# Attention, low-rank mixer and feed-forward on one core: the first batch's mixer moved a stage later, loads and DMA transposes moved earlier, and some transposes moved to TensorE

## The chip, the cores and the metric

The kernel runs on one core of a Trainium2 chip. The metric is device time in microseconds (us). Each timed comparison runs the kernel before and the variant on the same chip, in rounds. Here "slow" means more than 1.5% above the fastest run of the same kernel. The experiments ran on four chips (e1 to e4 on one, e5 to e8, e9 to e11 and e12 on others); the kernel before, timed again on each, had medians between 281.69 and 282.17 us, so a difference between runs of two chips carries about 0.5 us of doubt besides the spread. The engines are called PE (TensorE matmul), PEld (TensorE weight load), DVE (VectorE), ACT (ScalarE), POOL (GpSimd) and SP (SyncE, which here only issues DMAs).

## The reference

Four batches of eight-head attention over 768 positions, head size 64. Each query keeps 96 local positions and 8 global ones. The output, 768 x 512 per batch, goes through a rank-32 mixer along the sequence and a feed-forward block of width 2048.

```python
scores = scale * q @ k.T + bias;  scores = where(keep, scores, -1e9)
x = softmax(scores) @ v                      # (B, S, 512), heads side by side
h = x.transpose(0, 2, 1) @ U @ V             # U: 768x32, V: 32x768
u = x + h.transpose(0, 2, 1)
out = u + maximum(u @ w_ch1, 0) @ w_ch2      # w_ch1: 512x2048, w_ch2: 2048x512
```

## The kernel before

It works on 16 *pairs* of heads, four per batch. For pair i it needs: q and k transposed; `kP`, a copy of k in which 32 of each block's 128 positions are the global ones; `vp`, the same for v; scores, exp and mask; the products with v (`ob`); the mixer (`tmp_ps`, then `h_ps`, then `uu`, which is u in fp16); and `uT`, u transposed, for the feed-forward (`hps` then `cps`). Feed-forward work is cut into chunks of 512 tokens and queued. In the main loop (pairs 4 to 15) `fill(f)` takes f items of four products from the queue and puts them between the attention steps. In the traces here each engine takes its instructions in the order of the program (in the kernel before, GpSimd's `kP` copy of pair 5 starts only at 53.9 us, after the two loads listed ahead of it, at 51.66 and 52.47). So the place of a line decides what stands behind what.

Pairs 0 to 5 have q and k transposed by TensorE. Pairs 6 to 15 have it done by DMA transposes, issued on SP, from natural-layout staging tiles `qkn`. GpSimd issues all loads from DRAM; they convert fp32 to fp16.

```python
stg = stp.tile([P, NSB, 2, D], FP16, name="qkn", tag="qkn", bufs=4)
# v_prev: blocks of v with the global rows in front
if i < 2:  nc.vector.tensor_copy(vp, vh[:, :, 0:NPB]); ...   # VectorE
else:      nc.sync.dma_start(vp[G:P], vh[G:P, :, 0:NPB]); ...  # DMA, SBUF to SBUF
# ... cut ...
for i in range(NPAIR, NP):             # main loop, pairs 4..15
    v_prev(i + 2)
    scores(i + 1, 0);  fill(f)
    av(i);  norm(i)
    transposes(i + 2, 0);  fill(f)     # DMA transpose of q
    scores(i + 1, 1);  cast_x(i);  fill(f)
    mask(i + 1, 0);  mix_tmp(i);  fill(f)
    scores(i + 1, 2);  fill(f)
    mix_h(i, nc.vector);  mask(i + 1, 1)
    transposes(i + 2, 1);  k_prev(i + 2, nc.gpsimd);  fill(f)
    if i % 2 == 0 and i + 4 < NP:  load(i + 4, 2)
    fill(f)
    mix_t(i)                           # DMA transpose of u
    if i % NPAIR == NPAIR - 1:  queue_batch(i // NPAIR)
    fill(f)
while mlp_q:  fill(1)
```

The softmax here doesn't subtract the row's maximum and nothing guards it: scores larger than these inputs give would overflow.

Of the kernel before, what the change touches and what calls it, by code (L numbers as in the profile page):

```python
# [9 lines left out]
FP32 = mybir.dt.float32  # L10
# [7 lines left out]
def kernel(  # L18
# [27 lines left out]
    NPAIR = H // 2  # L46
    TT = 512
    D1 = D + 1
    KEEP = False
    DT = True  # L50
    assert NG <= G and NL <= P - G + 1 and NPAIR == NDC
    qk_scale = 1.0 / math.sqrt(D)
# [28 lines left out]

    w1_16 = big.tile([P, NDC, DFF], FP16, name="w1_16")
    w2_16 = big.tile([P, NJC, DM], FP16, name="w2_16")
    uT = big.tile([P, NDC, B * S], FP16, name="uT")
    VR = 8
    VPR = 3
    v16 = big.tile([P, VR, 2, NSB, D1], FP16, name="v16")
# [28 lines left out]
    def load_qk_natural(i):  # L116
        b, hp = divmod(i, NPAIR)
        for which, src in enumerate((q, k)):
            stg = stp.tile([P, NSB, 2, D], FP16, name="qkn", tag="qkn", bufs=4)
            for hi in range(2):  # L120
                nc.gpsimd.dma_start(  # L121
                    stg[:, :, hi],
                    src[b, 2 * hp + hi].rearrange("(n p) d -> p n d", p=P),
                )
            stage[i, which] = stg

    def load(i0, n):
        if DT and i0 >= NSTART:
            for j in range(n):
                load_qk_natural(i0 + j)  # L130
        else:
            load_qk(i0, n)
        load_v(i0, n)

    w1v = moe_w_ch1.rearrange("(c p) n -> p c n", p=P)
    w2v = moe_w_ch2.rearrange("(c p) n -> p c n", p=P)
# [48 lines left out]
        relf, relf, 0.5 - NL, BIG, op0=ALU.is_lt, op1=ALU.mult,  # L185
    )
    nc.vector.tensor_tensor(r12, r12, relf, ALU.add)
    nc.vector.tensor_copy(rel3[:, 0], rel3[:, 1])
    nc.vector.tensor_scalar_max(rel3[0:NG, 0], rel3[0:NG, 1], float(-NL))
    nc.vector.memset(rel3[0:G, 2], BIG)  # L190
    nc.vector.memset(rel3[0:NG, 2], float(-NL))
    expb = cst.tile([P, H, 3, P], FP16, name="expb")

    def masks_of(hp):
# [2 lines left out]



    def keep_busy(bank, n):  # L200
        for _ in range(n if KEEP else 0):
            nc.tensor.matmul(bank, zz[:, 0:P], zz, start=True, stop=True)

    qTs, kTs, kPs = {}, {}, {}
    probs = {}
# [5 lines left out]
    def transposes(i, which):  # L211
        if i >= NP:
            return
        stg = stage.pop((i, which))
        if DT and i >= NSTART:
            dst = qkp.tile([P, NSB, P], FP16, name="qkT", tag="qT" if which == 0 else "kT")
            nc.sync.dma_start_transpose(dst, stg.rearrange("p n h d -> p (n h d)"))
            if which == 0:
                qTs[i] = dst.rearrange("p n c -> p (n c)")
            else:  # L220
                kTs[i] = dst
            return
        if i < NSTART:
            bank = ps_mm("tpb")
            keep_busy(bank, 8 if i == 0 and which == 0 else 1)
            tp = bank.bitcast(FP16)[:, 0:NSB * P]
        else:
            tp = ps_tp("tp", FP16, NSB * P)
        for sb in range(NSB):
            for hi in range(2):  # L230
                nc.tensor.matmul(  # L231
                    tp[64 * hi:64 * hi + 64, sb * P:(sb + 1) * P], stg[:, hi, sb],
                    ident16, is_transpose=True,
                    start=(sb == 0), stop=(sb == NSB - 1),
                )
        tv = tp.rearrange("p (n c) -> p c n", n=NSB)
        if which == 0:
            qT = qkp.tile([P, S], FP16, name="qT", tag="qT")
            nc.scalar.activation(qT.rearrange("p (c n) -> p c n", n=NSB), tv, AF.Copy)
            qTs[i] = qT  # L240
        else:
            kT = qkp.tile([P, NSB, P], FP16, name="kT", tag="kT")
            ko = kT.rearrange("p n c -> p (n c)").rearrange("p (c n) -> p c n", n=NSB)
            if i == 0:
                nc.vector.tensor_copy(ko, tv)
            else:
                nc.scalar.activation(ko, tv, AF.Copy)
            kTs[i] = kT
# [10 lines left out]
    def v_prev(i):  # L259
        if i >= NP:  # L260
            return
        vh = v16[:, i % VR]
        vp = vp16[:, i % VPR]
        if i < 2:
            nc.vector.tensor_copy(vp, vh[:, :, 0:NPB])
            nc.vector.tensor_copy(vp[0:G], vh[0:G, :, 0:1].broadcast_to((G, 2, NPB, D1)))
        else:
            nc.sync.dma_start(vp[G:P], vh[G:P, :, 0:NPB])
            for hi in range(2):
                nc.sync.dma_start(  # L270
                    vp[0:G, hi], vh[0:G, hi, 0:1].broadcast_to((G, NPB, D1))
                )
# [5 lines left out]
    def scores(i, ci):  # L278
        if i >= NP:
            return  # L280
        qT, kT, kP = qTs[i], kTs[i], kPs.get(i)
        if ci == 0:
            probs[i] = epp.tile([P, 2, NBK, P], FP16, name="ep", tag="ep")
        ep = probs[i]
        idx = CH[ci]
        n = len(idx)
        scs = [ps_sc("sc") for _ in range(2)]
        if i < NPAIR:
            keep_busy(scs[0], 1)
        for j, bi in enumerate(idx):  # L290
            prev, t = ORDER[bi]
            for hi in range(2):
                r = slice(64 * hi, 64 * hi + 64)
                lhsT = kP[r, t - 1] if prev else kT[r, t]
                nc.tensor.matmul(  # L295
                    scs[hi][:, j * P:(j + 1) * P], lhsT, qT[r, t * P:(t + 1) * P],
                    start=(j == 0), stop=(j == n - 1),
                )
        for hi in range(2):
            nc.scalar.activation(  # L300
                ep[:, hi, idx[0]:idx[0] + n].rearrange("p n c -> p (n c)"),
                scs[hi][:, 0:n * P], AF.Exp, scale=qk_scale,
            )
# [89 lines left out]
    def mix_t(i):  # L393
        b, hp = divmod(i, NPAIR)
        uu = u16s.pop(i)
        if DT and i >= NPAIR:
            nc.sync.dma_start_transpose(
                uT[:, hp, b * S:(b + 1) * S].rearrange("p (n c) -> p n c", n=NSB),
                uu.rearrange("p n c -> p (n c)"),
            )  # L400
            return
        tpu = ps_tp("tpu", FP16, S)
        for st in range(NSB):
            nc.tensor.matmul(
                tpu[:, st * P:(st + 1) * P], uu[:, st], ident16, is_transpose=True,
                start=(st == 0), stop=(st == NSB - 1),
            )
        nc.vector.tensor_copy(uT[:, hp, b * S:(b + 1) * S], tpu)

    mlp_q = deque()  # L410

    def queue_chunk(ci):
        htr = ffp.tile([P, NJC, TT], FP16, name="htr", tag="htr")
        t0 = ci * TT

        def mk_jt(jt):
            def go():
                hh = ps_mm("hps")
                for dc in range(NDC):
                    nc.tensor.matmul(  # L420
                        hh, w1_16[:, dc, jt * P:(jt + 1) * P], uT[:, dc, t0:t0 + TT],
                        start=(dc == 0), stop=(dc == NDC - 1),
                    )
                if jt % 2 == 0:
# [7 lines left out]
        def mk_tt(tt, part):  # L432
# [13 lines left out]
                    nc.sync.dma_start(out[b, n * P:(n + 1) * P, :], osb)  # L446
            return go

        for jt in range(NJC):
            mlp_q.append(mk_jt(jt))  # L450
        for tt in range(TT // P):
# [6 lines left out]
                mlp_q.popleft()()  # L458


    transposes(0, 0)
    transposes(0, 1)
    masks_of(0)
    k_prev(0, nc.vector)
    scores(0, 0)
    transposes(1, 0)
    scores(0, 1)
    transposes(1, 1)
    mask(0, 0)
    scores(0, 2)  # L470
    masks_of(1)
    k_prev(1, nc.vector)
    v_prev(0)
    mask(0, 1)
    for i in range(NPAIR):
        last = i == NPAIR - 1
        v_prev(i + 2)
        scores(i + 1, 0)
        av(i)
        norm(i)  # L480
        scores(i + 1, 1)
        cast_x(i)
        mask(i + 1, 0)
        if i == 0:
            v_prev(1)
        transposes(i + 2, 0)
        if i > 0:
            mix_t(i - 1)
        mix_tmp(i)
        scores(i + 1, 2)  # L490
        if last:
            mix_h(i, nc.vector)
            mask(i + 1, 1)
            transposes(i + 2, 1)
            k_prev(i + 2, nc.gpsimd)
            mix_t(i)
        else:
            transposes(i + 2, 1)
            k_prev(i + 2, nc.vector if i == 0 else nc.gpsimd)
            mask(i + 1, 1)  # L500
            mix_h(i, nc.vector)
            if i + 2 < NPAIR:
                masks_of(i + 2)
        if i == 0:
            load(4, 2)
        if i == 1:
            load_w2()
        if i == 2:
            load(6, 2)

    def queue_batch(b):
        for ci in range(B * S // TT):
# [5 lines left out]
    for i in range(NPAIR, NP):  # L518
        if i % NPAIR == 0:
            f = max(1, len(mlp_q) // (8 * NPAIR))  # L520
        v_prev(i + 2)
        scores(i + 1, 0)
        fill(f)
        av(i)
        norm(i)
        transposes(i + 2, 0)
        fill(f)
        scores(i + 1, 1)
        cast_x(i)
        fill(f)  # L530
        mask(i + 1, 0)
        mix_tmp(i)
        fill(f)
        scores(i + 1, 2)
        fill(f)
        mix_h(i, nc.vector if DT else nc.gpsimd)
        mask(i + 1, 1)
        transposes(i + 2, 1)
        k_prev(i + 2, nc.gpsimd)
        fill(f)  # L540
        if i % 2 == 0 and i + 4 < NP:
            load(i + 4, 2)
        fill(f)
        mix_t(i)
        if i % NPAIR == NPAIR - 1:
            queue_batch(i // NPAIR)
        fill(f)
# [37 lines left out]
```

## Time and profile before

| quantity (kernel before) | value |
|---|---|
| time | 280.97 us median of the first three runs |
| stage 1, to the second scores of pair 5 | 54.8 us |
| stage 2, attention mixed with feed-forward | 55 to 220 us |
| stage 3, the last 256 feed-forward products | 220 to 276 us, 216 ns each |
| TensorE waits in stage 2, summed | about 23 us |

The first view is the table of busy time in chosen stretches, kernel before. The columns are the stretch, its length, then for PE, PEld, DVE, ACT and POOL the busy us and the number of instructions, then the granted clock, DMA share and GB/s.

```profile
core 0: us, PE busy (x) PEld busy (x) DVE busy (x) ACT busy (x) POOL busy (x), PEclk, DMA share, GB/s
13.00:55.00 42.00, 31.01 (x390) 21.28 (x390) 26.54 (x50) 26.20 (x48) 15.87 (x20) 0.92 1.47 190
55.00:220.00 165.00, 142.06 (x1123) 67.18 (x1120) 85.75 (x138) 58.81 (x107) 41.41 (x56) 0.99 0.87 104
220.00:280.00 60.00, 55.94 (x253) 24.52 (x252) 16.60 (x24) 9.55 (x16) 0.00 (x0) 0.99 0.11 40
```

In stage 1 no compute engine is full, and the DMA share is above 1 (transfers overlap). In stage 2 TensorE is busy for 142 of 165 us, and no other engine comes close, so the 23 us it lacks are what a change can win. Stage 3 is full.

The next view is the chain of waits, kernel before, at the end of stage 1: start, length, what.

```profile
33.37 18.01 DMA w_16_82<-in_moe_w_ch_dram
51.38 0.28 issue
51.66 0.70 POOL qkn L121
52.36 0.11 issue
52.47 1.43 POOL v_84 L110
53.91 0.59 POOL kP L255
54.50 0.26 POOL kP L256
...
54.80 0.33 PE sc L295 x4
```

The scores wait for `kP`. `kP` stands on GpSimd behind a load, and the issue of that load waits until the second half of w2 has landed. The load does not use w2; w2 is only the load that was issued eight places earlier.

The third view is the TensorE timeline, kernel before, cut to some waits of stage 2: start, length, engine, line, operation, output and inputs, shapes, count, and in brackets the idle time before it and what ended it.

```profile
66.06 0.40 PE L295 MATMUL sc<-qkT 64*128 64x128 f16 x8 [2.79 <-DMA qkT<-qkn]
...
91.50 0.52 PE L295 MATMUL sc<-qkT 64*128 64x128 f16 x8 [3.55 <-DMA qkT<-qkn]
91.95 1.89 PE L438 MATMUL cps<-w_16_82,htr 128*128 128x512 f16 x4
...
98.20 0.29 PE L367 MATMUL tmp_ps<-x_1302,u_106 128*32 128x128 f16 x6 [0.93 <-ACT x_1302 L359]
...
106.19 1.24 PE L420 MATMUL hps<-uT,w_16_81 128*128 128x512 f16 x5 [0.99 <-DMA uT<-uu]
...
220.24 1.02 PE L420 MATMUL hps<-uT,w_16_81 128*128 128x512 f16 x4 [1.24 <-DMA uT<-uu]
```

The change aims at three families of waits: for transposed q/k, for the cast of x on ScalarE, and for transposed u. (A fourth, for results that ScalarE and VectorE must first take away, `htr`, is about 5 us and stays.) After the 3.55 us wait four products took 1.89 us, at a granted clock of 0.50 between 92 and 94 us; undisturbed groups of four took 1.04. Below, "cold" means such products at the half clock.

### The profile page before, as it was taken

To read this page: it belongs to the slowest core of one execution; us is meant where nothing else is said; L and a number is where in the kernel's file an instruction comes from. 1 tells how busy PE (TensorE), PEld (TensorE's weight loads), DVE (VectorE), ACT (ScalarE), POOL (GpSimd) and SP (SyncE) were. 2 spreads that over 40 slices of the span, in tenths; PEclk is the share of its full clock that TensorE was granted. 3 is DMA by queue.
4 is the path that set the end of the run, shared out by engine and by line. 5 is a ranking of instruction groups with operands and counts; after the bars stand their busy time and mean duration, and the time that the engine had idled before them with its cause. 6 is when DMAs were issued, how large, how long until landed. Compare 5 with 4: busy or idle time off the path is not lost.

```text
span 280.0 us, 4506 instructions
## 1 busy us (share of the span) xinstructions
PE 234.0 (84%) x1832; PEld 116.4 (42%) x1832; DVE 134.0 (48%) x226; ACT 100.6 (36%) x180; POOL 68.9 (25%) x96
## 2 busy tenths in 40 slices
PE   2567786976785898999999999678989899999994
PEld 1355564433342444444444444334444344444441
DVE  4366657363644263735457345455665332223221
ACT  2776665343541325433064230446321131013100
POOL 8930436405440534052402423111000000000000
PEclk9999998699999799999999999999999999999999
DMA  8999999977994999597593985954113200120011
GB/s 85 160 196 215 188 194 199 135 66 124 112 129 117 147 136 136 51 156 80 117 135 82 127 74 137 119 109 81 28 46 97 66 2 0 75 76 2 0 75 75
DMA packets 99796, 29.08 MB, mean 104 GB/s; under 512 B 88256, under 2 KB 96192, under 8 KB 99776
## 3 DMA queue, kind: packets, MB, share of 16 engines
q0 software_dynamic: 62736, 13.73, 55.9%
q1 hardware_dynamic: 37040, 15.07, 24.8%
q8 instruction: 14, 0.23, 0.3%
q14 instruction: 6, 0.05, 0.1%
HBM read 27.46 MB, written 6.29 MB: 121 GB/s over the span
## 4 chain that ended last, share of the span: by engine, by line
PE 59%; DMA 15%; ACT 11%; DVE 7%; POOL 3%; issue 2%; SPq 2%; DVEq 0%; ACTq 0%; POOLq 0%
PE cps L438 24%; PE hps L420 24%; DMA w_16_82<-in_moe_w_ch_dram 6%; ACT ep L300 6%; PE sc L295 4%; DMA uT<-uu 3%; DMA qkT<-qkn 3%; DVE x_sb L386 2%; DMA qkst<-in_q_dram 2%; DVE ep L313 2%; PE ob L333 2%; PE ob L337 2%; PE tmp_ps L367 1%; PE h_ps L381 1%; ACT htr L425 1%
## 5 line engine op out<-in xcount | busy, mean ns | idle before, releaser
L420 PE MATMUL hps<-uT,w_16_81 128*128 128x512 f16 x384 | 93.8, 384 | 8.2 <-DMA uT<-uu 3.4
L438 PE MATMUL cps<-w_16_82,htr 128*128 128x512 f16 x384 | 89.7, 382 | 0.0
L300 ACT ACTIVATE ep<-sc 128x512 f16<-128x512 f32 (+1 forms) x96 | 48.8, 561 | 85.2 <-PE sc L295 85.2
L420 PEld LDWEIGHTS <-w_16_81 128*128 128x128 f16 x384 | 35.2, 98 | 49.8 <-issue 13.9
L427 DVE TENSOR_SCALAR htr<-hps 128x512 f16<-128x512 f32 x48 | 33.1, 690 | 41.2 <-PE hps L420 41.2
L438 PEld LDWEIGHTS <-htr 128*128 128x128 f16 x384 | 35.3, 98 | 40.2 <-issue 0.9
L425 ACT ACTIVATE htr<-hps 128x512 f16<-128x512 f32 x48 | 28.7, 598 | 63.7 <-PE hps L420 63.1
L313 DVE TENSOR_TENSOR ep<-ep,expb 128x1280 f16<-128x1280 f16 x32 | 26.6, 833 | 15.6 <-ACT ep L300 15.6
L445 DVE TENSOR_TENSOR osb<-cps,x_sb 128x512 f32<-128x512 f32 x24 | 16.6, 690 | 34.8 <-PE cps L438 34.8
L121 POOL DMA_DIRECT2D qkn<-in_k_dram x20 | 16.6, 842 | 23.0 <-DMA qkT<-qkn 17.7
L255 POOL COPY kP<-qkT 128x480 f16<-128x480 f16 x10 | 6.3, 634 | 64.4 <-DMA qkT<-qkn 58.6
L121 POOL DMA_DIRECT2D qkn<-in_q_dram x20 | 17.0, 860 | 17.0 <-DMA qkT<-qkn 17.0
L386 DVE TENSOR_TENSOR x_sb<-x_sb,h_ps 128x768 f32<-128x768 f32 x16 | 15.2, 952 | 11.6 <-PE h_ps L381 11.6
L349 DVE RECIPROCAL rcp<-ob 128x12 f32<-128x12 f32 x16 | 3.7, 233 | 30.1 <-PE ob L337 30.1
L333 PE MATMUL ob<-vp_85,ep 128*128 128x65 f16 x160 | 15.5, 212 | 1.1 <-DVE ep L313 1.1
L231 PE MATMUL tpb<-ident_93,qkst 128*64 128x128 f16 x144 | 9.9, 306 | 7.3 <-DMA qkst<-in_q_dram 6.7
L350 DVE TENSOR_TENSOR x_sb<-ob,rcp 128x768 f32<-128x768 f32 x16 | 15.3, 957 | 0.6
L337 PE MATMUL ob<-v_84,ep 128*128 128x65 f16 x160 | 15.5, 212 | 0.0
L333 PEld LDWEIGHTS <-ep 128*128 128x128 f16 x160 | 13.5, 110 | 4.4 <-issue 1.6
L337 PEld LDWEIGHTS <-ep 128*128 128x128 f16 x160 | 13.6, 111 | 0.0
L295 PE MATMUL sc<-qkT 64*128 64x128 f16 x120 | 7.0, 223 | 7.6 <-DMA qkT<-qkn 7.6
L110 POOL DMA_DIRECT2D v_84<-in_v_dram x9 | 12.3, 1370 | 0.0
(116 smaller groups left out, 151.9 us busy)
## 6 DMA issues: line engine op xcount, KB each, us to landing
out_dram<-osb SPq DMA_DIRECT2D x24, 256.0 KB, 2.1
v_84<-in_v_dram POOLq DMA_DIRECT2D x7, 384.0 KB, 7.7
w_16_81<-in_moe_w_ch_dram POOLq DMA_DIRECT2D x2, 1024.0 KB, 17.6
w_16_82<-in_moe_w_ch_dram POOLq DMA_DIRECT2D x2, 1024.0 KB, 15.2
qkn<-in_q_dram POOLq DMA_DIRECT2D x20, 96.0 KB, 3.6
qkn<-in_k_dram POOLq DMA_DIRECT2D x20, 96.0 KB, 5.3
vp_85<-v_84 SPq DMA_DIRECT2D x14, 121.9 KB, 2.4
qkst<-in_q_dram POOLq DMA_DIRECT2D x2, 384.0 KB, 14.3
```

The lines of the kernel that those rows point to most:

```text
L121: nc.gpsimd.dma_start(stg[:, :, hi], src[b, 2 * hp + hi].rearrange("(n p) d -> p n d", p=P),)
L295: nc.tensor.matmul(scs[hi][:, j * P:(j + 1) * P], lhsT, qT[r, t * P:(t + 1) * P], start=(j == 0), stop=(j == n - 1),)
L300: nc.scalar.activation(ep[:, hi, idx[0]:idx[0] + n].rearrange("p n c -> p (n c)"), scs[hi][:, 0:n * P], AF.Exp, scale=qk_scale,)
L313: nc.vector.tensor_tensor(blk, blk, eb[:, :, m:m + 1].broadcast_to((P, 2, NPB, P)), ALU.mult,)
L333: nc.tensor.matmul(ob[:, t], ep[:, hi, NSB + t - 1], vp16[:, i % VPR, hi, t - 1], start=True, stop=False,)
L337: nc.tensor.matmul(ob[:, t], ep[:, hi, t - 1], v16[:, i % VR, hi, t], start=False, stop=True,)
L386: nc.vector.tensor_tensor(xp, xp, hps[:, 0:S].rearrange("p (n c) -> p n c", n=NSB), ALU.add)
L420: nc.tensor.matmul(hh, w1_16[:, dc, jt * P:(jt + 1) * P], uT[:, dc, t0:t0 + TT], start=(dc == 0), stop=(dc == NDC - 1),)
L425: nc.scalar.activation(htr[:, jt], hh, AF.Relu)
L427: nc.vector.tensor_scalar_max(htr[:, jt], hh, 0.0)
L438: nc.tensor.matmul(cps, htr[:, jc, tt * P:(tt + 1) * P], w2_16[:, jc], start=(jc == 0), stop=(jc == NJC - 1),)
L445: nc.vector.tensor_tensor(osb, cps, xs[b][:, n], ALU.add)
```

## The change

Its intent is to fill TensorE's waits: loads and DMA transposes earlier with more staging room, one more `fill` between the cast and the product that needs it, u of the last pair of a batch transposed by TensorE, and in stage 1 a mixer one stage later, with zero products to keep TensorE's clock up. Keeping u for two batches only makes room for the staging tiles, but it forces some fills early (`release_u`), before the old u is overwritten. The core of the diff:

```diff
-    KEEP = False
+    KEEP = True
-    uT = big.tile([P, NDC, B * S], FP16, name="uT")
+    uT = big.tile([P, NDC, 2 * S], FP16, name="uT")
-  ... tag="qkn", bufs=4)
+  ... tag="qkn", bufs=8)
     def load(i0, n):
         if DT and i0 >= NSTART:
+            load_v(i0, n)
             for j in range(n):
                 load_qk_natural(i0 + j)
         else:
             load_qk(i0, n)
-        load_v(i0, n)
+            load_v(i0, n)
 # v_prev
-        if i < 2:
+        if i == 0:
             nc.vector.tensor_copy(vp, vh[:, :, 0:NPB])
 # mix_t
-        if DT and i >= NPAIR:
+        if DT and i >= NPAIR and hp < NPAIR - 1:
             nc.sync.dma_start_transpose(...)
 # stage 1 (cut): keep_busy(n) calls; mix_h(i - 1) at the head of iteration i;
 # k_prev(i + 2) always on gpsimd; v_prev(1) before the first scores
 # main loop
+        if i % 2 == 0 and i + 4 < NP:
+            load(i + 4, 2)
+        transposes(i + 2, 0)
+        transposes(i + 2, 1)
         v_prev(i + 2)
         scores(i + 1, 0)
         ...
         mask(i + 1, 0)
+        fill(f)
         mix_tmp(i)
-        fill(f)
         scores(i + 1, 2)
         fill(f)
-        mix_h(i, nc.vector if DT else nc.gpsimd)
+        mix_h(i, nc.vector)
         mask(i + 1, 1)
-        transposes(i + 2, 1)
         k_prev(i + 2, nc.gpsimd)
         fill(f)
-        if i % 2 == 0 and i + 4 < NP:
-            load(i + 4, 2)
-        fill(f)
-        mix_t(i)
+        release_u(i // NPAIR)
+        if i % NPAIR < NPAIR - 1:
+            mix_t(i)
+        fill(f)
+        if i % NPAIR == NPAIR - 1:
+            mix_t(i)
```

More of the change, by code (lines that the diff above doesn't have):

```diff
@@ L118, in load_qk_natural @@
         for which, src in enumerate((q, k)):
-            stg = stp.tile([P, NSB, 2, D], FP16, name="qkn", tag="qkn", bufs=4)
+            stg = stp.tile([P, NSB, 2, D], FP16, name="qkn", tag="qkn", bufs=8)
             for hi in range(2):
@@ L187, with rel_globals @@
     nc.vector.tensor_tensor(r12, r12, relf, ALU.add)
-    nc.vector.tensor_copy(rel3[:, 0], rel3[:, 1])
-    nc.vector.tensor_scalar_max(rel3[0:NG, 0], rel3[0:NG, 1], float(-NL))
-    nc.vector.memset(rel3[0:G, 2], BIG)
-    nc.vector.memset(rel3[0:NG, 2], float(-NL))
+    def rel_globals():
+        nc.vector.tensor_copy(rel3[:, 0], rel3[:, 1])
+        nc.vector.tensor_scalar_max(rel3[0:NG, 0], rel3[0:NG, 1], float(-NL))
+        nc.vector.memset(rel3[0:G, 2], BIG)
+        nc.vector.memset(rel3[0:NG, 2], float(-NL))
     expb = cst.tile([P, H, 3, P], FP16, name="expb")
@@ L196, in masks_of, with keep_busy @@
             nc.scalar.activation(expb[:, h], rel3, AF.Exp, scale=slope[h])
-    def keep_busy(bank, n):
-        for _ in range(n if KEEP else 0):
-            nc.tensor.matmul(bank, zz[:, 0:P], zz, start=True, stop=True)
+    def keep_busy(n):
+        if KEEP and n:
+            bank = ps_tp("dmy", FP32, 512)
+            for _ in range(n):
+                nc.tensor.matmul(bank, zz[:, 0:P], zz, start=True, stop=True)
     qTs, kTs, kPs = {}, {}, {}
@@ L224, in transposes @@
             bank = ps_mm("tpb")
-            keep_busy(bank, 8 if i == 0 and which == 0 else 1)
             tp = bank.bitcast(FP16)[:, 0:NSB * P]
@@ L287, in scores @@
         scs = [ps_sc("sc") for _ in range(2)]
-        if i < NPAIR:
-            keep_busy(scs[0], 1)
         for j, bi in enumerate(idx):
@@ L395, in mix_t @@
         uu = u16s.pop(i)
-        if DT and i >= NPAIR:
+        if DT and i >= NPAIR and hp < NPAIR - 1:
             nc.sync.dma_start_transpose(
-                uT[:, hp, b * S:(b + 1) * S].rearrange("p (n c) -> p n c", n=NSB),
+                uT[:, hp, b % 2 * S:b % 2 * S + S].rearrange("p (n c) -> p n c", n=NSB),
                 uu.rearrange("p n c -> p (n c)"),
@@ L401, in mix_t @@
             return
-        tpu = ps_tp("tpu", FP16, S)
+        if i < NPAIR:
+            tpu = ps_mm("tpub").bitcast(FP16)[:, 0:S]
+        else:
+            tpu = ps_tp("tpu", FP16, S)
         for st in range(NSB):
@@ L407, in mix_t @@
             )
-        nc.vector.tensor_copy(uT[:, hp, b * S:(b + 1) * S], tpu)
+        nc.vector.tensor_copy(uT[:, hp, b % 2 * S:b % 2 * S + S], tpu)
     mlp_q = deque()
+    reads_left = {}
     def queue_chunk(ci):
@@ L414, in queue_chunk @@
         t0 = ci * TT
+        r0 = t0 % (2 * S)
         def mk_jt(jt):
             def go():
+                reads_left[ci] -= 1
                 hh = ps_mm("hps")
@@ L420, in go @@
                     nc.tensor.matmul(
-                        hh, w1_16[:, dc, jt * P:(jt + 1) * P], uT[:, dc, t0:t0 + TT],
+                        hh, w1_16[:, dc, jt * P:(jt + 1) * P], uT[:, dc, r0:r0 + TT],
                         start=(dc == 0), stop=(dc == NDC - 1),
@@ L447, in mk_tt @@
             return go
+        reads_left[ci] = NJC
         for jt in range(NJC):
@@ L458, in fill @@
                 mlp_q.popleft()()
+    keep_busy(15)
     transposes(0, 0)
     transposes(0, 1)
+    k_prev(0, nc.vector)
+    rel_globals()
+    v_prev(0)
+    v_prev(1)
+    keep_busy(3)
+    scores(0, 0)
     masks_of(0)
-    k_prev(0, nc.vector)
-    scores(0, 0)
+    keep_busy(2)
     transposes(1, 0)
@@ L470 @@
     scores(0, 2)
+    k_prev(1, nc.vector)
+    mask(0, 1)
     masks_of(1)
-    k_prev(1, nc.vector)
-    v_prev(0)
-    mask(0, 1)
+    keep_busy(2)
     for i in range(NPAIR):
-        last = i == NPAIR - 1
         v_prev(i + 2)
+        if i > 0:
+            mix_h(i - 1, nc.vector)
         scores(i + 1, 0)
+        transposes(i + 2, 0)
+        scores(i + 1, 1)
+        keep_busy(2)
         av(i)
         norm(i)
-        scores(i + 1, 1)
+        scores(i + 1, 2)
         cast_x(i)
         mask(i + 1, 0)
-        if i == 0:
-            v_prev(1)
-        transposes(i + 2, 0)
+        transposes(i + 2, 1)
+        keep_busy(3)
+        k_prev(i + 2, nc.gpsimd)
         if i > 0:
             mix_t(i - 1)
+        mask(i + 1, 1)
+        keep_busy(3)
         mix_tmp(i)
-        scores(i + 1, 2)
-        if last:
-            mix_h(i, nc.vector)
-            mask(i + 1, 1)
-            transposes(i + 2, 1)
-            k_prev(i + 2, nc.gpsimd)
-            mix_t(i)
-        else:
-            transposes(i + 2, 1)
-            k_prev(i + 2, nc.vector if i == 0 else nc.gpsimd)
-            mask(i + 1, 1)
-            mix_h(i, nc.vector)
-            if i + 2 < NPAIR:
-                masks_of(i + 2)
+        if i + 2 < NPAIR:
+            masks_of(i + 2)
         if i == 0:
@@ L509, with release_u @@
             load(6, 2)
+    mix_h(NPAIR - 1, nc.vector)
+    keep_busy(6)
+    mix_t(NPAIR - 1)
+    def release_u(b):
+        for ci in reads_left:
+            while ci * TT < (b - 1) * S and reads_left[ci]:
+                fill(1)
     def queue_batch(b):
@@ L520 @@
             f = max(1, len(mlp_q) // (8 * NPAIR))
+        if i % 2 == 0 and i + 4 < NP:
+            load(i + 4, 2)
+        transposes(i + 2, 0)
+        transposes(i + 2, 1)
         v_prev(i + 2)
@@ L525 @@
         norm(i)
-        transposes(i + 2, 0)
         fill(f)
@@ L531 @@
         mask(i + 1, 0)
+        fill(f)
         mix_tmp(i)
-        fill(f)
         scores(i + 1, 2)
         fill(f)
-        mix_h(i, nc.vector if DT else nc.gpsimd)
+        mix_h(i, nc.vector)
         mask(i + 1, 1)
-        transposes(i + 2, 1)
         k_prev(i + 2, nc.gpsimd)
         fill(f)
-        if i % 2 == 0 and i + 4 < NP:
-            load(i + 4, 2)
+        release_u(i // NPAIR)
+        if i % NPAIR < NPAIR - 1:
+            mix_t(i)
         fill(f)
-        mix_t(i)
+        if i % NPAIR == NPAIR - 1:
+            mix_t(i)
         if i % NPAIR == NPAIR - 1:
```

## The prediction

> **What bounds the kernel now.** The table of stretches and the PE timeline show three stages. (1) 0 to 55 us, batch 0's attention: TensorE's instructions are short and cold (128x128 transposes 314 ns against 219 ns later), its DMA share is at or over 1.0 in every 10 us stretch, and the chain of waits runs through one wait of 18.0 us for the second half of w2 (lands at 51.4 us): GpSimd's eighth q/k load after w2 waits for it, and the kP copy of pair 5 is queued behind, so scores wait until 54.8. Loads bound this stage. (2) 55 to 220 us: attention of 12 pairs mixed with four chunks of the feed-forward; TensorE in program order bounds it. (3) 220 to 277: 256 products of 512 columns at 216 ns back to back, nothing to gain.
>
> In stage 2 TensorE's waits sum to about 23 us: DMA transposes of q/k (qkT) 2.79 + 3.55 + 0.42 + 0.89 = 7.7; the cast of x on ScalarE before tmp_ps, seven times 0.93 and once 0.52 = 7.0; DMA transposes of u at three batch ends 3.4; bank releases by htr (ScalarE, VectorE) about 5.
>
> **What the change does.**
> - Loads before everything else in an iteration, eight staging buffers, v first, transposes first: the GpSimd waits for freed staging (35 us in the waits view) go, and transposes are issued almost an iteration earlier. I expect the 7.7 us to fall under 1. With it goes a cold spell after the 3.55 us wait: at 92 us four products took 1.89 us instead of 1.04 and the 22 attention products 1.2 instead of 0.67, about 1.8 us in all. The Trainium skill ("TensorE: Matmul & The Clock Gate", HAM clock gate) says an idle window of about 3.4 us halves the clock; this trace agrees. Gain about 9.5 us.
> - One more fill (0.87 us) between cast_x and mix_tmp: the 0.93 us waits shrink to 0.1-0.2. Gain about 6 us.
> - Last pair's u transposed on TensorE: costs about 0.34 us of TensorE and a 0.55 us VectorE copy instead of a 2.7-4.0 us DMA; but forced early fills (release of u) leave the queue empty at the last two batch ends, so a bubble of about 1.2 us stays there. Gain about 1 us.
> - Keeping two batches of u only makes room: 0.
> - Stage 1: one period was 8.2 us, ScalarE alone needs about 6; the later mixer and warm zero products would allow 7.5. But q of pair 4 lands only at 34.7 us, and its transposes now stand earlier in TensorE's order, so TensorE waits there; w2 still lands near 51 us and kP of pair 5 still stands behind it. After the loop a chain of mixer, cast, transpose and copy (3.5 us) is no longer overlapped. Net gain 0.5 us, between -2 and +3.
>
> Sum: about 17 us, all on TensorE's chain of stage 2. **Predicted 264 us, range 258 to 270. Faster by over 2%: 0.96, within 2%: 0.03, slower: 0.01.**
>
> **What would show it.** Waits of sc on qkT under 1 us in total; tmp_ps waits for x under 0.3 us each; hps waits on uT's DMA gone, replaced by waits on a VectorE copy under 1 us at two of three batch ends; the main loop's pair-5 scores still at 53-55 us; w2 still landing at 50-52 us; a long TensorE wait for qkst before 35 us; the last stage still 55-56 us long; the zero products change nothing in the time.
>
> **What would make it wrong.** Stage 1 not bound by loads in the way I read it; kP of pair 6, now behind nine load issues on GpSimd (about 8 us), stalling scores; mix_h starved of its cast with one fill fewer before it; earlier loads colliding with the DMA transposes.

## The result

The changed kernel takes 269.41 us (median of four fast runs, 267.73 to 270.75); the kernel before took 281.37 us beside it. The ratio is 0.9565, 95% interval 0.9495 to 0.9634. A ratio is the mean time of one kernel's fast runs over that of the other's in the same rounds, so it is not quite the ratio of the medians. The profiled run is the fastest of the four, with a span of 265.7 us.

The table of stretches of the changed kernel, with stages cut at its own borders:

```profile
13.00:58.00 45.00, 32.62 (x424) 19.52 (x424) 24.11 (x44) 25.38 (x48) 15.95 (x22) 0.85 1.49 184
58.00:205.00 147.00, 139.41 (x1136) 67.11 (x1137) 85.27 (x140) 58.59 (x107) 41.90 (x58) 1.00 0.95 112
205.00:266.00 61.00, 56.87 (x262) 24.96 (x258) 17.47 (x26) 9.55 (x16) 0.00 (x0) 0.99 0.10 39
```

Stage 2 shrank to 147 us, of which TensorE works 139. Stage 1, however, became longer. From the second scores of pair 5 to the end, the spans give 280.0 - 54.8 = 225.2 us before and 265.7 - 58.35 = 207.35 after: 17.85 us won. Stage 1 lost 58.35 - 54.80 = 3.55 us. The chain of waits of the changed kernel shows where:

```profile
14.82 0.62 SPq L274
15.44 0.04 issue
15.48 15.33 DMA vp_85<-v_84
...
44.04 12.31 DMA v_84<-in_v_dram
56.34 0.28 issue
56.63 0.08 POOL qkn L121
...
57.44 0.60 POOL kP L259
58.04 0.25 POOL kP L260
```

And the TensorE timeline of the changed kernel, all its waits for `vp` and `kP`, then some of those left in stage 2:

```profile
27.81 0.23 PE L335 MATMUL ob<-vp_85,ep 128*128 128x65 f16 x1 [3.65 <-DMA vp_85<-v_84]
...
30.85 0.22 PE L335 MATMUL ob<-vp_85,ep 128*128 128x65 f16 x1 [2.26 <-DMA vp_85<-v_84]
...
58.35 0.29 PE L297 MATMUL sc<-qT,kP 64*128 64x128 f16 x4 [2.12 <-POOL kP L260]
...
76.54 0.40 PE L297 MATMUL sc<-qkT 64*128 64x128 f16 x8 [0.34 <-DMA qkT<-qkn]
...
166.77 1.24 PE L428 MATMUL hps<-uT,w_16_81 128*128 128x512 f16 x5 [0.64 <-DVE uT L413]
...
204.78 0.51 PE L409 MATMUL tpu<-ident_93,uu 128*128 128x128 f16 x6 [0.85 <-DVE uu L392]
```

The `vp` copy of pair 1, which VectorE had made in under 1 us, is now three DMAs from SBUF to SBUF: a large one (121.9 KB), and a small one (20.3 KB) with the global rows of each of the two heads. The large one was issued at 14.1 us and took 10.1 us. The two small ones took 12.9 and 15.3 us, the second from 15.5 to 30.8 us, and these two are what TensorE waited for. Everything behind it, the issue of w2 included (35.25 us instead of 32.16), came late. The waits for the cast are gone from the list altogether, and the waits for transposed q/k fell from 7.7 us to 0.34.

The second loss is at `kP` of pair 5. The GpSimd timeline of the changed kernel:

```profile
53.94 0.82 POOL L121 DMA_DIRECT2D qkn<-in_k_dram  x1 [3.56 <-DMA w_16_82<-in_moe_w_ch_dram]
56.63 0.82 POOL L121 DMA_DIRECT2D qkn<-in_k_dram  x1 [1.87 <-DMA v_84<-in_v_dram]
57.44 0.60 POOL L259 COPY kP<-kT 128x480 f16<-128x480 f16 x1
```

There are two waits where there had been one. With v first, the load issued eight places before the last k load is v itself, which lands at 56.3 us.

### The profile page after: what moved, and what is told of

It is laid out like the page before. It is cut to its first block, busy times and chain, and to the rows that moved or that the text cites. A ratio compares the mean times of both kernels' runs of the same rounds, so it can differ in the third digit from the quotient of the medians.

```text
span 265.7 us, 4667 instructions
## 1 busy us (share of the span) xinstructions
PE 239.0 (90%) x1910; PEld 116.0 (44%) x1910; DVE 133.7 (50%) x225; ACT 99.7 (38%) x180; POOL 69.5 (26%) x98
## 4 chain that ended last, share of the span: by engine, by line
PE 61%; DMA 16%; ACT 7%; POOL 5%; DVE 5%; issue 3%; SPq 1%; DVEq 0%; POOLq 0%; ACTq 0%
PE cps L446 27%; PE hps L428 23%; DMA vp_85<-v_84 6%; DMA v_84<-in_v_dram 5%; ACT ep L302 4%; PE sc L297 4%; DMA qkT<-qkn 4%; POOL qkn L121 2%; DVE x_sb L388 2%; DMA v16w<-in_moe_V_dram 2%; PE h_ps L383 1%; PE ob L335 1%; POOL v_84 L110 1%; PE ob L339 1%; PE tmp_ps L369 1%
## 5 line engine op out<-in xcount | busy, mean ns | idle before, releaser
L428 PE MATMUL hps<-uT,w_16_81 128*128 128x512 f16 x384 | 91.4, 379 | 5.5 <-ACT htr L433 3.2
L446 PE MATMUL cps<-w_16_82,htr 128*128 128x512 f16 x384 | 88.6, 379 | 0.0
L453 DVE TENSOR_TENSOR osb<-cps,x_sb 128x512 f32<-128x512 f32 x24 | 16.5, 689 | 30.7 <-PE cps L446 30.6
L388 DVE TENSOR_TENSOR x_sb<-x_sb,h_ps 128x768 f32<-128x768 f32 x16 | 15.3, 953 | 14.1 <-PE h_ps L383 14.1
L207 PE MATMUL dmy<-zz 128*128 128x512 f16 x60 | 19.6, 454 | 1.3 <-DVE zz L149 1.2
L335 PE MATMUL ob<-vp_85,ep 128*128 128x65 f16 x160 | 13.5, 199 | 5.9 <-DMA vp_85<-v_84 5.9
L352 DVE TENSOR_TENSOR x_sb<-ob,rcp 128x768 f32<-128x768 f32 x16 | 15.3, 958 | 0.6
L335 PEld LDWEIGHTS <-ep 128*128 128x128 f16 x160 | 11.8, 102 | 5.9 <-DMA vp_85<-v_84 4.0
L339 PE MATMUL ob<-v_84,ep 128*128 128x65 f16 x160 | 13.5, 199 | 0.0
L339 PEld LDWEIGHTS <-ep 128*128 128x128 f16 x160 | 11.7, 101 | 2.4 <-issue 2.4
L392 DVE CAST uu<-x_sb 128x768 f16<-128x768 f32 x16 | 9.6, 600 | 0.6
## 6 DMA issues: line engine op xcount, KB each, us to landing
vp_85<-v_84 SPq DMA_DIRECT2D x15, 121.9 KB, 6.5
```

The costliest lines, as they stand in the source:

```text
L207: nc.tensor.matmul(bank, zz[:, 0:P], zz, start=True, stop=True)
L335: nc.tensor.matmul(ob[:, t], ep[:, hi, NSB + t - 1], vp16[:, i % VPR, hi, t - 1], start=True, stop=False,)
L339: nc.tensor.matmul(ob[:, t], ep[:, hi, t - 1], v16[:, i % VR, hi, t], start=False, stop=True,)
L388: nc.vector.tensor_tensor(xp, xp, hps[:, 0:S].rearrange("p (n c) -> p n c", n=NSB), ALU.add)
L428: nc.tensor.matmul(hh, w1_16[:, dc, jt * P:(jt + 1) * P], uT[:, dc, r0:r0 + TT], start=(dc == 0), stop=(dc == NDC - 1),)
L446: nc.tensor.matmul(cps, htr[:, jc, tt * P:(tt + 1) * P], w2_16[:, jc], start=(jc == 0), stop=(jc == NJC - 1),)
```

## The experiments

All twelve gave correct results. Theory A was: stage 2's gain is as predicted, and stage 1 lost because urgent small work (the `vp` copy, the `kP` copy) stands behind loads. The first rival was: stage 1 is bound by the total of the loads, whatever the small work does; the second: the stage-1 changes help, and the lost time lies elsewhere. Times are medians; the fast-run means are in the text where a difference is taken.

| run | change from | median us | fast runs, mean us | ratio, 95% interval |
|---|---|---|---|---|
| e1 | the changed kernel again | 269.38 | 268.55 | 0.9525 (0.9443 to 0.9607) |
| e2 | changed kernel | 265.18 | 265.33 | 0.9411 (0.934 to 0.9481) |
| e3 | changed kernel | 268.97 | 268.93 | 0.954 (0.9472 to 0.9609) |
| e4 | changed kernel | 266.66 | 266.76 | 0.9462 (0.9395 to 0.9528) |
| e5 | kernel before | 289.06 | 284.91 | 1.0114 (1.0013 to 1.0215) |
| e6 | e2 | 273.63 | 273.65 | 0.9714 (0.966 to 0.9769) |
| e7 | e2 | 275.56 | 275.46 | 0.9779 (0.9724 to 0.9833) |
| e8 | e2 | 271.63 | 271.63 | 0.9643 (0.9582 to 0.9703) |
| e9 | e2 | 280.19 | 280.10 | 0.993 (0.9854 to 1.0006) |
| e10 | e9 | 279.74 | 278.98 | 0.9901 (0.9811 to 0.9991) |
| e11 | e2 | 265.27 | 265.16 | 0.941 (0.9342 to 0.9479) |
| e12 | e2 | 264.57 | 263.75 | 0.9396 (0.9333 to 0.9458) |

### e1: the changed kernel again

> The changed kernel again, unaltered, as the yardstick for the other runs on this chip. Both theories: 267.5 to 271 us, with the TensorE wait of the attention products of pair 1 for the copied V blocks (vp) of several us near 24 us.

It took 266.91 to 272.04 us, with waits for `vp` of 3.96 and 1.72 us in its profile. That profile fell on a slow run and is used for no comparison. The spread is much wider than that of e6 (273.54 to 273.78), so single profiles of the changed kernel may differ by 2 us or more (its fast runs here span 266.91 to 269.98).

### e2: the V blocks of pair 1 on VectorE

```diff
-        if i == 0:
+        if i < 2:
             nc.vector.tensor_copy(vp, vh[:, :, 0:NPB])
 # and v_prev(1) moved from before the first scores to iteration 0, after mask(1, 0)
```

> The V blocks of pair 1 (vp) are copied by VectorE, where the kernel before had it, instead of by DMA. Theory A (the DMA copy, queued among the startup loads, cost the startup its gain): the wait near 24 us goes, the second half of w2 is issued about 3 us earlier or more, pair 5's second scores start at about 54 to 55 us instead of 58.35, and the time falls by 3 to 5 us, to about 265. Theory B (loads bound the startup whatever TensorE waits for): w2 still lands near 53 us, the time stays within 1 us of the changed kernel's.

All four runs (264.06 to 266.91) are at or below the lowest fast run of e1 on the same chip; the means differ by 3.2 us, though the two intervals overlap. The TensorE timeline of e2, its two longest waits of stage 1:

```profile
35.01 0.85 PE L235 MATMUL tpb<-ident,qkst 128*64 128x128 f16 x12 [5.04 <-DMA qkst<-in_q_dram]
...
56.78 0.29 PE L297 MATMUL sc<-qT,kP 64*128 64x128 f16 x4 [1.15 <-POOL kP L260]
```

The wait for `vp` is gone, and the wait for q of pair 4 that the prediction had foreseen appears in its place: the load lands just before 35 us. So the copy did cost time, but part of it would have been lost to the loads anyway. Theory A stands in its direction; its "54 to 55 us" for pair 5 does not (56.78).

### e3: no zero products

```diff
-    KEEP = True
+    KEEP = False
```

> The changed kernel without the zero products. Theory A (startup is bound by loads and one DMA copy): within 1 us of the changed kernel. Rival (a warm TensorE shortens each startup period): 3 us slower or more, with transposes of 314 ns in place of 219 and a later second half of w2.

The means are 268.93 against 268.55: no difference. The products do raise TensorE's clock in stage 1 (the median transpose takes 219 ns in the changed kernel, 314 in the one before), but warm transposes wait for the same loads. That the zero products are the reason for the 219 ns is seen in e3, where the median is 314 again. The granted clock does not show it: it reads 1.00 from 0 to 40 us in the kernel before, whose transposes take 314 ns, so in stage 1 the durations are the better sign.

### e4: the startup section of the kernel before

The edit puts the stage-1 code of the kernel before in front of the changed main loop and keeps the changed loads.

> The changed main loop and loads behind the startup section of the kernel before, without zero products. Theory A (all the gain is made in the main loop, and the new startup lost about 3.5 us of it): about 264 us, some 17 us below the kernel before, second scores of pair 5 at about 54.5 us. Rival (the new startup is itself worth something, its late start is made up later): 269 us or more.

Both theories' times were missed: it lies between them. It is 1.8 us faster than e1 and 1.4 us slower than e2 by the means. So the new startup is worth a little once its `vp` copy is mended, and costs something as it is; both differences are small beside the spreads. One line of its TensorE timeline is worth more than the time:

```profile
57.10 0.29 PE L297 MATMUL sc<-qT,kP 64*128 64x128 f16 x4 [3.35 <-POOL kP L260]
```

With the old startup these scores began at 54.80 in the kernel before, and about 54.5 had been expected here. What stands ahead of their `kP` on GpSimd differs only in the order within the loads. Of GpSimd's waits here, 4.89 us are for w2 and 2.34 for v: v first costs pair 5 about 2.3 us (57.10 - 54.80, from one profile each).

### e5: the loads alone, in the kernel before

The edit puts the prefetch part of the diff (v first, eight buffers, u of two batches with `release_u`, loads and transposes at the iteration's start) into the kernel before, and nothing else. So it tests the loads together with the forced fills that make their room.

> The kernel before with only the prefetch part of the change: v first, eight staging buffers, u of two batches (which makes their room) with its forced fills, loads and DMA transposes at the start of an iteration; the fills, the startup's order and the DMA transposes of u stay as before. Theory A: the waits of scores for transposed q/k (7.7 us) and the cold spell (1.8 us) go, at most 2 to 3 us are given back at the second scores of pair 5 because v first adds a wait on GpSimd; net 5 to 9 us, so 272.5 to 276.5 us. Rival (TensorE only meets the next wait, on the cast of x or on u): under 3 us gained.

Missed: 283.2 and 286.61 us in the fast runs, 291.52 and 292.83 in the slow ones, so no gain at all. The profile is of a slow run; I read from it only what waits, not how long it would be in a fast run. Its waits for transposed q/k are almost gone (one of 0.46 us). In their place, at each batch end:

```profile
106.73 2.29 PE L424 MATMUL hps<-uT,w 128*128 128x512 f16 x5 [5.70 <-DMA uT<-uu]
```

The other two are 3.86 and 3.96 us. At this first end the DMA transpose of u was issued at 99.51 us and took 7.2 us to land in this slow run (3.0 in the fast profile of the kernel before), among loads now issued from 97.7 us on. This fits the "earlier loads colliding with the DMA transposes" that the prediction had listed, but not priced; the loads were not moved to test it.

The other two ends are a different case. Their DMA transposes landed in 2.8 us each (4.0 and 2.7 in the kernel before), and no load was issued near them. What is missing is work to put in front of the wait. The second batch end, first in the kernel before, then in e5:

```profile
168.73 5.34 PE L438 MATMUL cps<-w_16_82,htr 128*128 128x512 f16 x24
...
176.33 0.38 PE L420 MATMUL hps<-uT,w_16_81 128*128 128x512 f16 x1 [1.18 <-DMA uT<-uu]
```

```profile
174.11 1.89 PE L442 MATMUL cps<-w,htr 128*128 128x512 f16 x8
175.84 0.81 PE L424 MATMUL hps<-uT,w 128*128 128x512 f16 x3
180.51 2.29 PE L424 MATMUL hps<-uT,w 128*128 128x512 f16 x5 [3.86 <-DMA uT<-uu]
```

Between the last mixer product of the batch and the products that need the transposed u, the kernel before has 24 feed-forward products from the queue, and e5 has 8; at the third end there are 12 and 4, at the first end 12 in both. Counting the queue in the two programs says why: in e5 `release_u` forces four items in pair 8, and the queue is then empty before the transposes of the last two batch ends, where the kernel before still has two items and one.

### e6: the second fill put back

```diff
         mask(i + 1, 0)
-        fill(f)
         mix_tmp(i)
+        fill(f)
```

> As e2 (V blocks of pair 1 on VectorE), but the second fill between the cast of x and the tmp_ps products goes back behind tmp_ps. Theory A: the seven waits of 0.93 us for the cast in the two one-fill batches come back, 5 to 7 us slower than e2, about 271 us. Rival (the slack before mix_h or elsewhere takes it up): within 2 us of e2.

It is 273.65 - 265.33 = 8.3 us slower than e2, more than expected. The waits are back, seven of 0.93 us and one of 0.52, for example:

```profile
70.94 0.29 PE L369 MATMUL tmp_ps<-x,u 128*32 128x128 f16 x6 [0.93 <-ACT x L361]
```

Their sum is 7.0 us. The rest is close to what the profile's modelled ends hide: a product counts as busy for 384 ns though the next one may start 216 ns after it, so each wait costs up to 168 ns more than its bracket says. Eight times that is an estimated 1.3 us, and 7.0 + 1.3 = 8.3.

### e7: the last pair's u by DMA

```diff
-        if DT and i >= NPAIR and hp < NPAIR - 1:
+        if DT and i >= NPAIR:
```

> As e2, but the last pair's u is transposed by DMA again. Theory A: each of the three batch ends waits 1 to 3 us for the DMA instead of about 0 to 1 us; 2 to 5 us slower than e2 in all, more than the 1 us that I predicted, since the queue is empty at the last two batch ends. Rival (prediction): 1 us slower, within the noise.

It is 10.1 us slower than e2 by the fast runs, far more than either theory said. The profile is of a slow run, and shows the kind of wait:

```profile
171.28 2.29 PE L428 MATMUL hps<-uT,w 128*128 128x512 f16 x5 [3.86 <-DMA uT<-uu]
...
215.53 14.70 PE L428 MATMUL hps<-uT,w 128*128 128x512 f16 x53 [3.94 <-DMA uT<-uu]
```

Five products in 2.29 us instead of 1.24 (the same group after 166.77 in the changed kernel) are cold ones, so each wait of nearly 4 us is paid again in clock. The two DMA transposes landed in 2.8 and 2.7 us, so these are the waits of an empty queue, as in e5, and not of slowed transposes. At the first batch end, where loads are about (landing 4.3 us), the wait for u is 0.84 us. There are also waits of 1.18 and 1.45 us for transposed q/k. How the 10.1 us divide among these in a fast run I did not measure.

### e8: the loads of pairs 6 and 7 later

```diff
-        if i == 2:
-            load(6, 2)
 # and in iteration 3, behind k_prev(5):
+        if i == 3:
+            load(6, 2)
```

> As e2, but the loads of pairs 6 and 7 are issued after the kP copy of pair 5 instead of before it, so that this copy no longer stands behind the GpSimd waits for w2 and for v. Theory A: the wait of the second scores of pair 5 for kP (1.15 us in e2, 2.1 to 3.4 elsewhere) goes; q/k of pair 6 come up to 3 us later but were ahead; 1 to 2 us faster than e2, about 263.5 us. Rival (later loads come back as a wait for the transposed q/k of pair 6): the same as e2 or slower.

The rival was right: 6.3 us slower than e2. The wait for `kP` is gone, and one for transposed q/k of pair 6 has taken its place, longer than what it freed:

```profile
66.30 0.60 PE L297 MATMUL sc<-qkT 64*128 64x128 f16 x8 [5.44 <-DMA qkT<-qkn]
```

### e9 and e10: loads in the order of use

```diff
     load(2, 2)
+    load(4, 2)
     load_w1()
 # in stage 1: load(6, 2) in iteration 2; load_w2() in iteration 3, behind kP of pair 5
```

> As e2, but the loads are put in the order of their use: pairs 4 and 5 before w1, pairs 6 and 7 before w2, and w2 only after the kP copy of pair 5. Theory A (startup is bound by the order in the load queue, not by its total): the 5 us wait for q of pair 4 near 35 us goes, the main loop starts at 46 to 49 us instead of 52 to 53, and the time is 258 to 261 us. Rival (the total of the loads binds, or w2 arrives too late for the second products, or the loads of pairs 8 and 9 do): 264 us or more.

> As e9 without the zero products. Theory A (once loads no longer bind the startup, its period is set by TensorE, ScalarE and VectorE in turn, and a cold TensorE adds to it): 1 to 3 us slower than e9. Rival (the zero products never matter here): within 1 us of e9.

Missed by 20 us. The wait for q of pair 4 is gone, but others have come (TensorE timeline of e9):

```profile
34.90 0.24 PE L336 MATMUL ob<-vp,ep 128*128 128x65 f16 x1 [4.04 <-DMA vp<-v]
...
38.07 0.22 PE L336 MATMUL ob<-vp,ep 128*128 128x65 f16 x1 [2.38 <-DMA vp<-v]
...
80.05 0.40 PE L298 MATMUL sc<-qkT,kP 64*128 64x128 f16 x4 [13.69 <-POOL kP L261]
```

The `vp` copy of pair 2 is now the one that is late, and `kP` of pair 6 stands behind loads that wait for the two halves of w2 and for v (5.47, 6.30 and 5.68 us on GpSimd). The startup was therefore not bound by the order of the loads alone. e10, without zero products, is 1.1 us faster than e9 by the means, with overlapping intervals: the zero products are not shown to help here either, though this pair is no clean test, since the loads still bind it.

### e11: v after q and k for pairs 6 and 7 alone

```diff
+            if i0 > NSTART:  load_v(i0, n)
             for j in range(n):  load_qk_natural(i0 + j)
+            if i0 == NSTART:  load_v(i0, n)
```

> As e2, but for pairs 6 and 7 alone v is loaded after q and k, as the kernel before had it. Theory A (v first makes GpSimd wait a second time, for v's landing, ahead of the kP copy of pair 5): the wait for v goes, kP comes about 2 us earlier, the 1.15 us wait of the second scores of pair 5 goes, up to 1.2 us faster than e2. Rival (the next wait takes its place: transposed q/k of pair 6 or kP of pair 6): no change or slower.

The second wait on GpSimd goes and pair 5's scores start at 53.50 us, 3.3 us earlier than in e2. The median is the same as e2's (265.27 and 265.18). Pair 6 now waits 1.01 us for its `kP`. What else takes the rest is not visible from one profile each, and the spread of both runs is 2 to 3 us, so this stays open.

### e12: the small copies on VectorE, loads in the order of use

```diff
-        if i == 0:                     # v_prev
+        if i < NPAIR:
-        k_prev(i + 2, nc.gpsimd)       # stage 1, and pair 6 in the main loop
+        k_prev(i + 2, nc.vector)
+    load(4, 2)                         # before load_w1()
 # load(6, 2) in iteration 0, load_w2() in iteration 1
```

> As e2, with what stood behind the load queue taken away from it: the V blocks of pairs 1 to 3 and the kP copies of pairs 2 to 6 go to VectorE, so that nothing urgent stands behind GpSimd's load issues or in the DMA queues; then pairs 4 and 5 are loaded before w1, pairs 6 and 7 before w2. Theory A (e9 lost to the DMA copies and to the kP copy of pair 6 behind w2, not to its order of loads): no wait for q of pair 4, vp or kP above 1 us, the main loop's second scores of pair 5 at 46 to 50 us instead of 53 to 57, time 258 to 262 us. Rival (the total of the loads before pair 8, or VectorE in the startup, binds): 264 us or more, with a new wait for transposed q/k or for VectorE.

The mechanism is as expected: no wait for `vp`, none of note for q of pair 4, and pair 5's second scores begin at 48.4 us without a wait, 8 us earlier than in e2. But the time is 264.57 us, 1.6 us below e2 by the means with overlapping intervals. The later stages take much of it back: from pair 5's scores to the end the profile has 211.9 us, against 207.5 in e2 (TensorE timeline of e12):

```profile
54.87 1.02 PE L429 MATMUL hps<-uT,w 128*128 128x512 f16 x4 [0.69 <-ACT htr L434]
57.05 0.40 PE L298 MATMUL sc<-qkT 64*128 64x128 f16 x8 [1.15 <-DMA qkT<-qkn]
58.09 1.86 PE L429 MATMUL hps<-uT,w 128*128 128x512 f16 x4 [0.64 <-DVE htr L436]
```

The DMA transposes of pair 6 meet the loads of w2 and of pair 8, and TensorE drops to its slow clock (granted clock 0.50 from 58 to 61 us). e2, e11 and e12 all beat both the kernel before and the changed kernel by the medians; among the three no order is shown.

## Why the prediction was right or wrong

The time lay inside the range, near its upper end (269.4 against 264, range 258 to 270). The sum was right because stage 2 was read correctly; stage 1 was not. Of the forecast 17 us, about 16.5 were to come from stage 2 and 0.5 from stage 1. The profiles show 17.85 won and 3.55 lost, so a slightly larger gain made up for a part of the loss.

- **Transposed q/k: right.** "Under 1 us" was predicted, 0.34 measured. But this gain cannot be had by this part alone: in e5 the loads with their forced fills win nothing, because waits for u take its place (a slower DMA transpose at the first batch end, an empty queue at the other two). What the loads would give without forced fills was not tested.
- **The cast of x: right in mechanism, too small in size.** 6 us were predicted, 8.3 measured (e6 against e2). The term left out the modelled ends of the products, and left 0.1 to 0.2 us each where nothing remained.
- **u on TensorE: the right size against the kernel before, the wrong role.** The waits left at the last two batch ends, 0.64 and 0.85 us, fit the bubble of about 1.2 us with the transposes added. As a part of the changed kernel it is worth 10.1 us (e7), not 1: it is what makes the forced fills, and so the earlier loads, affordable. How much of the 10.1 us is waiting and how much cold clock is not measured in a fast run.
- **Keeping two batches of u: the mechanism was named, its price was not.** The empty queue after forced fills, foreseen for the last two batch ends, is what exposes the waits for u there in e5 and e7 (3.9 us each, with transposes of 2.7 to 2.8 us).
- **Stage 1: wrong.** A net gain of 0.5 us (-2 to +3) was predicted; the profile shows a loss of 3.55. The failed steps: the move of the `vp` copy of pair 1 from VectorE to DMA was not costed at all (its small parts took 12.9 and 15.3 us to land; mending it gave 3.2 us by the means and 1.57 us at pair 5's scores by the profiles, e2); and v first was counted as a gain only, though it adds a wait to GpSimd's queue ahead of `kP` of pair 5 (2.3 us later in e4). "Second scores of pair 5 at 53 to 55" was therefore missed by over 3 us, and w2 came at 53.9 us, not 50 to 52. The wait for q of pair 4 was masked in the changed kernel by the waits for `vp` and appears in e2 as foreseen.
- **Zero products: right.** No change in the time is shown (e3).
- **Stage 3: right within 1 us.** From its first product at 205.12 to the last at 261.88 us, 56.8 us.
- **The named risks.** `kP` of pair 6 behind the load issues did not stall the changed kernel, but cost 13.69 us in e9. Starving `mix_h` is not seen in stage 2. A collision of loads and DMA transposes fits one wait of e5, at the first batch end; in e7, with the changed kernel's main loop, that end waits only 0.84 us. The dearer effect was the empty queue at the other two ends, and it is this that the transposes on TensorE avoid.

The arithmetic for the profiled run: 17.85 us won after pair 5's scores, 3.55 lost before, 14.3 in all, and 280.0 - 265.7 = 14.3. The medians differ by 12.0, mainly because the profiled run of the changed kernel was the fastest of its four (267.73 us), while that of the kernel before took 281.85.

The Trainium skill says in "DMA: Bandwidth & Descriptors", section "Issuing engines are not separate DMA queues", that DMAs from SP and GpSimd run on the same 16 DMA engines and interleave. It is the fact that I should have applied to the `vp` copy: the small parts of such copies land in a median of 2.9 us over the whole kernel before, and took 12.9 and 15.3 us among the startup loads of the changed kernel. The trace of the kernel before already held a warning: its slowest small part, issued in the startup, took 11.6 us. As for the skill's page "TensorE: Matmul & The Clock Gate", section on the HAM clock gate, its half clock after idle windows is seen after the waits for u of 3.86 to 5.70 us in e5 and e7: the granted clock is 0.50 just after each (e7: 2.29 us for five products instead of 1.24).

## What to carry to other kernels

Before moving a small copy to a DMA or to an engine that issues loads, look at what is in flight or queued there at that moment, not at its median duration. A change made of several parts is to be costed as a whole: here the early loads with their forced fills won nothing by themselves, and a part that seemed worth 1 us carried 10. When a wait grows, look first whether the transfer became slower or the work in front of the wait became less: here it was the work at two of three places. When a startup is bound by loads, taking one wait away mostly uncovers the next load; follow the chain through two or three of them before promising the gain.

## What the Trainium skill lacked or had wrong

- "TensorE: Matmul & The Clock Gate", section "Back-to-back issue gap", gives a sustained 131 ns for a product of 512 columns with its weight load. Here 64 such products in a row took 13.83 us, 216 ns each; the page's isolated formula (216 ns) fits, the sustained figure does not.
- The same page, part 4 on transposes, says that the full clock does not engage for transposes. Here the median transpose of q and k (128 columns moved, 64 weights) took 314 ns in the kernel before and in e3, and 219 ns in the changed kernel, where zero products ran ahead of it. Whether transposes alone would bring the full clock was not tested.
- The same page has no figure for how much idle time, cut into short pieces, brings the half clock. In e12 waits of 0.69, 1.15 and 0.64 us within 4 us, with work between them, were enough: four products then took 1.86 us instead of 1.04. Why is not shown.
- "DMA: Bandwidth & Descriptors", section "Latency and other measured facts", has a fixed cost of about 2 us and nothing on small SBUF-to-SBUF copies beside large loads: 12.9 and 15.3 us here for 20.3 KB each, with 2.9 us as the median of such copies in the kernel before.
- No page has it that a load issue on GpSimd waits for the landing of the load eight places before. In e12 eight load issues in a row each waited for exactly that one (for example 3.62 and 5.03 us for the halves of w1, then 3.16 for v). Whether program or hardware sets the eight is not shown.
